# Two transformer layers on one core: waits between PSUM banks of one tile dropped in the first and last stages, and MLP weight blocks loaded through GpSimd's queue

## The chip, the core and the metric

The kernel runs on one core of a Trainium2 chip. In this kernel TensorE (PE in the profile, PEld for its weight loads; 1688.4 us busy in the profile before) multiplies and writes to PSUM. ScalarE (ACT, 1751.8 us) and VectorE (DVE, 1172.0 us) read PSUM and work on SBUF. GpSimd (POOL) is busy for 2.4 us before the change. SyncE (SP) only issues transfers. The metric is the device time of one execution in microseconds, as a median of several executions; lower is better.

## The reference, cut to what matters

```python
x = A_x                                            # 1 x 2048 x 512, bf16
for _ in range(2):                                 # the same weights in both layers
    x = x + attention(layernorm(x), wqkv, wo)      # 32 heads of 16, softmax(q k^T / 4) v
    x = x + relu(layernorm(x) @ w1) @ w2           # 512 -> 1792 -> 512
```

Two layers of attention over 2048 tokens need 2 x 32 x 2048 x 2048 exponentials. They are what most of the time goes to: 1738.8 us of ScalarE in a span of 1836.0 us.

## The kernel before

The kernel plans its own order of instructions while it is being built: `work`, `urgent` and `evac` are lists of pending groups, each with an assumed cost, and the exponentials set the pace. The framework then adds the waits. It knows tiles, not banks: if one engine writes bank 1 of a tile while another still reads bank 0 of it, a wait is put between them (0.67 us of it at 1801.26 us in the profile before).

The kernel has eight banks of PSUM in use, in four tiles. Two tiles `ps_s` of three banks each hold attention scores; `ps_f` and `ps_o` have one bank each. In the first and last stages there are no scores yet, or none left, and those banks serve for everything else:

```python
    wide = [True]
    bank_no = [0]

    def bank():
        if not wide[0]:
            return ps_f[:]
        n = bank_no[0] % 7
        bank_no[0] += 1
        if n == 6:
            return ps_f[:]
        return ps_s[n // W][:, n % W, :]          # W = 3 banks of one tile
```

The first stage (head), after the first layernorm:

```python
    for i in range(TPC):                           # 4 rows of 128 tokens
        pt = ln_transpose(tag, i)                  # 4 TensorE transposes into bank()
        if i % 2:
            nc.scalar.copy(out=xnT[0][:, :, i * P : (i + 1) * P], in_=pt)
        else:
            nc.vector.tensor_copy(out=xnT[0][:, :, i * P : (i + 1) * P], in_=pt)
        mark(("xnT", tag, i))
        idle_matmuls(1)                            # a matmul whose result nobody reads
    ...
    b = plain(k_mms(0, 0))                         # K projection
    nc.scalar.copy(out=ktp[0][0][0][:], in_=b)
    ...
    urgent.append(q_group(None, 0, 0, 0, 0))       # Q projection, two masks on VectorE
    run_all()
    for kb in range(2):                            # V projections
        nc.scalar.copy(out=v_out(0, kb), in_=v_in(plain(v_mms(kb))))
```

In the middle each pair of heads is normalized by this chain. `u` holds 128 x 512 sums; four of its rows are the softmax denominators. They go to a compact tile `c` (8 KB), are inverted, go back into `u`, and are spread to all partitions as `r` (256 KB):

```python
        def copy():                                # u <- ps_o, then
                nc.sync.dma_start(out=c[:], in_=sums)
        def recip():
            nc.vector.reciprocal(out=c[:], in_=c[:])
            nc.sync.dma_start(out=sums, in_=c[:])
            nc.sync.dma_start(out=r[:], in_=bass.AP(tensor=sums.tensor, ...))   # each row 32 times
        def mul(a, w):                             # ot <- u * mask * r
```

The W1 blocks come through SyncE's queue, four buffers deep:

```python
            nc.sync.dma_start(
                out=w1buf[n % NW1][:],
                in_=B_w1[:, ft * P : (ft + 1) * P].rearrange("(c p) f -> p c f", p=P),
            )
```

The last stage (tail), after the last exponential: out-projection of the last 512 tokens, layernorm, transposes, the MLP with 14 W1 groups, store.

```python
    for i in rows:
        last_steps[0](i)
        add(banks[i], ot[NT - 1][:, i * P : (i + 1) * P], wo[:, (NT - 1) // 2, :], False, True)
        nc.scalar.copy(out=x[:], in_=banks[i])
    ...                                            # layernorm
    for i in rows:
        pt = ln_transpose(tag, i, more[i])
        ...                                        # copies to xn2T by both engines
    for ft in range(NF + 1):
        ...                                        # W1 group ft, ReLU, W2 group ft - 1
    for i in rows:
        ...                                        # last copies, stores
```

The softmax here doesn't subtract the row's maximum and nothing guards it: scores larger than these inputs give would overflow.

## Time and profile before

Median 1838.3 us of four runs (1836.8 to 1839.36); the profiled execution has a span of 1836.0 us.

| stretch | from | to | length |
|---|---|---|---|
| head, until the first exponential | 0 | 18.48 | 18.5 us |
| middle, ScalarE full of exponentials | 18.48 | 1781.13 | 1762.7 us |
| tail | 1781.13 | 1836.0 | 54.9 us |

Only time taken out of the head, out of ScalarE's gaps in the middle, or out of the tail counts. The prediction below shows the lines for that. One more view matters for the tail: stretches of the trace cut at the edges where the granted TensorE clock changes. The columns are the stretch and its length, then busy time and instructions of PE, PEld, DVE, ACT and POOL, then the granted clock (1.00 is full), the DMA share and GB/s.

```profile
1795.65:1799.06 3.41, 0.00 (x0) 0.00 (x0) 3.00 (x14) 0.19 (x1) 0.00 (x0) 0.50 0.00 0
1799.06:1802.47 3.41, 1.24 (x9) 0.91 (x10) 2.15 (x8) 0.58 (x1) 0.00 (x0) 0.50 0.00 0
1802.47:1805.89 3.42, 3.20 (x14) 1.74 (x15) 0.42 (x1) 0.58 (x1) 0.00 (x0) 0.50 0.00 0
```

In the traces of the two kernels the clock changes only at edges that lie a whole number of 3.41 us apart (nine changes in each). TensorE stands during the layernorm, in the first stretch. In the second it is busy for just 1.24 us: the transposes are waiting for copies out of neighbouring banks. The third, with 3.20 us of work, is still at half clock; only after it does the clock return (1.00 in the stretch 1805.9 to 1810 us).

### The profile page before, as it was taken

What the parts mean: (1) busy time and instruction counts of PE and PEld (TensorE: products, weight loads), DVE (VectorE), ACT (ScalarE), POOL (GpSimd) and SP (SyncE); (2) the same over time, 40 slices, a digit from 0 to 9 for tenths busy, and PEclk for the clock granted to TensorE, in tenths of its full rate; (3) what the DMA queues carried; (4) which work ended last, traced back from release to release, by engine and by line L of the source; (5) the groups of instructions that cost most, each with busy time, mean ns of one, the idle gap of its engine ahead of it and who ended that gap; (6) DMA issues with size and microseconds to landing.
All of it is one profiled execution on the core that took longest, in us unless ns stands there. A gap on an engine that the chain in (4) does not pass through costs nothing.

```text
span 1836.0 us, 31204 instructions
## 1 busy us (share of the span) xinstructions
PE 1688.4 (92%) x13535; PEld 533.9 (29%) x13709; DVE 1172.0 (64%) x1795; ACT 1751.8 (95%) x1388; POOL 2.4 (0%) x35
## 2 busy tenths in 40 slices
PE   8899999999999999999999888999999999999996
PEld 2223332222232222322222321232222222232223
DVE  7437668677676876778432323586678668666673
ACT  6989999999999999999999997999999999999981
POOL 0000000000000000000000000000000000000000
PEclk9999999999999999999999996999999999999998
DMA  4000000110002000110010001001000110001101
GB/s 144 1 10 11 18 15 8 39 26 11 10 19 46 9 13 11 25 38 13 13 27 15 1 18 27 13 19 42 16 21 8 33 36 16 13 13 41 25 19 40
DMA packets 92749, 42.37 MB, mean 23 GB/s; under 512 B 76612, under 2 KB 84548, under 8 KB 92612
## 3 DMA queue, kind: packets, MB, share of 16 engines
q1 hardware_dynamic: 91268, 39.06, 9.4%
q8 instruction: 107, 1.75, 0.4%
q10 hardware_dynamic: 1344, 1.31, 0.2%
q14 instruction: 30, 0.25, 0.0%
HBM read 20.71 MB, written 2.10 MB: 12 GB/s over the span
## 4 chain that ended last, share of the span: by engine, by line
ACT 82%; PE 11%; DVE 4%; DMA 2%; issue 1%; SPq 0%; DVEq 0%; ACTq 0%
ACT e L934 82%; PE ps_s L911 4%; PE ps_o L701 3%; PE ps_f L360 2%; PE ps_s L984 1%; DMA c<-u 1%; DVE dy L772 1%; DVE di L742 1%; DVE de L772 0%; DMA r<-u 0%; DVE dm L766 0%; DVE q L503 0%; PE ps_f L984 0%; DVE vaug L496 0%; DVE stats L379 0%
## 5 line engine op out<-in xcount | busy, mean ns | idle before, releaser
L934 ACT ACTIVATE e<-ps_s 128x1536 bf16<-128x1536 f32 (+1 forms) x1366 | 1738.8, 1520 | 23.9 <-PE ps_s L911 23.0
L911 PE MATMUL ps_s<-q,ktp 32*128 32x512 bf16 x7287 | 778.2, 384 | 99.2 <-ACT e L934 77.2
L701 PE MATMUL ps_o<-e,vaug 128*32 128x512 bf16 x3860 | 547.0, 393 | 5.6 <-DVE u L647 4.5
L911 PEld LDWEIGHTS <-ktp 32*128 32x128 bf16 x7287 | 232.7, 92 | 530.9 <-issue 460.8
L701 PEld LDWEIGHTS <-vaug 128*32 128x32 bf16 x4568 | 162.8, 93 | 493.5 <-issue 467.1
L742 DVE TENSOR_SCALAR di<-ps_s 128x512 int32<-128x512 f32 x236 | 162.1, 688 | 93.1 <-PE ps_s L911 90.5
L772 DVE SCALAR_TENSOR_TENSOR de<-dy,di 128x1024 bf16<-128x1024 f32 x118 | 144.3, 1223 | 9.1 <-PE ps_o L701 2.4
L772 DVE SCALAR_TENSOR_TENSOR dy<-dm 128x1024 f32<-128x1024 f32 x118 | 144.1, 1221 | 2.5
L772 DVE SCALAR_TENSOR_TENSOR dy<-dy,dm 128x1024 f32<-128x1024 f32 x118 | 144.1, 1221 | 2.1
L545 DVE TENSOR_SCALAR ht<-ps_f 128x512 bf16<-128x512 f32 x98 | 67.5, 689 | 107.8 <-PE ps_f L360 102.0
L360 PE MATMUL ps_f<-xn2T,w 128*128 128x512 bf16 x346 | 114.3, 384 | 5.8 <-issue 1.9
L360 PE MATMUL ps_f<-w,ht 128*128 128x512 bf16 x349 | 110.6, 384 | 4.1 <-issue 3.0
L660 DVE SCALAR_TENSOR_TENSOR ot<-u,mask,r 128x512 bf16<-128x512 f32 (+1 forms) x67 | 46.5, 694 | 69.4 <-DMA r<-u 69.3
L766 DVE TENSOR_SCALAR di<-di 128x1024 int32<-128x1024 int32 x118 | 81.6, 692 | 3.1
L503 DVE TENSOR_SCALAR q<-ps_f,qmask 128x512 bf16<-128x512 f32 x78 | 55.7, 745 | 42.8 <-PE ps_f L360 40.9
L701 PE MATMUL ps_o<-de,vaug 128*32 128x512 bf16 x472 | 82.9, 383 | 0.0
L766 DVE TENSOR_SCALAR dm<-di 128x1024 int32<-128x1024 int32 x118 | 81.3, 689 | 1.5
L360 PE MATMUL ps_f<-xnT,wqkv 128*128 128x512 bf16 x235 | 78.0, 389 | 4.4 <-issue 2.3
L360 PE MATMUL ps_f<-wo,ot 128*128 128x512 bf16 x195 | 63.9, 385 | 2.9 <-issue 2.2
L701 PE MATMUL ps_o<-di,vaug 128*32 128x512 bf16 x236 | 57.7, 391 | 0.0
L649 DVE COPY u<-ps_o 128x512 f32<-128x512 f32 x48 | 33.1, 690 | 30.2 <-PE ps_o L701 30.1
L468 DVE CAST ktp<-ps_f 128x512 bf16<-128x512 f32 x31 | 21.4, 690 | 44.4 <-PE ps_f L360 38.2
(89 smaller groups left out, 517.4 us busy)
## 6 DMA issues: line engine op xcount, KB each, us to landing
r<-u SPq DMA_DIRECT2D x63, 256.0 KB
w<-in_B_w_dram SPq DMA_DIRECT2D x112, 128.0 KB
out_dram<-x SPq DMA_DIRECT2D x16, 128.0 KB
x<-in_A_x_dram SPq DMA_DIRECT2D x14, 128.0 KB
w<-in_B_w_dram SPq DMA_DIRECT2D x1, 1792.0 KB
wqkv<-in_A_wqkv_dram ACTq DMA_DIRECT2D x2, 512.0 KB
c<-u SPq DMA_DIRECT2D x63, 8.0 KB
u<-c SPq DMA_DIRECT2D x63, 8.0 KB
```

The costliest lines, as they stand in the source:

```text
L360: nc.tensor.matmul(b, lhsT, rhs, start=(i == 0), stop=(i == n - 1))
L468: nc.vector.tensor_copy(out=ktp[l][T][j][:], in_=b)
L503: nc.vector.tensor_scalar(out=qbuf[n % 2][e][:], in0=b, scalar1=qmask[e][:, 0:1], scalar2=None, op0=ALU.mult,)
L545: nc.vector.tensor_scalar(out=ht[ft], in0=b, scalar1=0.0, scalar2=None, op0=ALU.max)
L649: nc.vector.tensor_copy(out=u[:], in_=ps_o[:])
L660: nc.vector.scalar_tensor_tensor(out=ot[t][:, a : a + w], in0=u[:, a : a + w], scalar=mask[e][:, 0:1], in1=r[:, a : a + w], op0=ALU.mult, ...
L701: nc.tensor.matmul(ps_o[32 * g : 32 * g + 32, :], vaug[sg["l"]][kb][:, 4 * sg["T"] + g, 2 * e : 2 * e + 32], rhs, start=g not in sg["begun ...
L742: first = nc.vector.tensor_scalar(out=di[:, half, :].bitcast(I32), in0=src, scalar1=EXP_BIAS, scalar2=0.0, op0=ALU.add, op1=ALU.max,)
L766: nc.vector.tensor_scalar(out=out[:].bitcast(I32), in0=di[:].bitcast(I32), scalar1=keep, scalar2=put, op0=ALU.bitwise_and, op1=ALU.bitwise_or,
L772: nc.vector.scalar_tensor_tensor(out=out[:], in0=x[:], scalar=c, in1=y[:], op0=ALU.add, op1=ALU.mult)
L911: nc.tensor.matmul(b[:, w, :], kt[32 * g : 32 * g + 32, kc : kc + P], qbuf[sg["n"] % 2][sg["e"]][32 * g : 32 * g + 32, :], start=True, sto ...
L934: ex = nc.scalar.activation(out=eb[:, :m, :], in_=b[:, :m, :], func=ACTF.Exp, scale=1.0 / (LOG2E * UNIT),)
```

## The change

The intent: drop, in head and tail, the waits between different banks of one tile, and take the 112 W1 loads off SyncE's queue. A helper logs which bank each instruction touches, and tells the framework that an earlier user of another bank of that tile is no dependency. An exception is made where the order comes from data (`needs`). The head's Q projection is written out with the same helper, so the plan of the first 32 us changes a little.

```diff
+    def uses(ins, bank, makes=None, needs=None):
+        tile, w = bank
+        log = users.setdefault(tile, deque(maxlen=40))
+        for other, ow, made_there in log:
+            if (
+                ow != w and other.engine != ins.ins.engine
+                and (needs is None or made_there != needs)
+            ):
+                tc.declare_no_dep(ins.ins, other, reason="different PSUM banks")
+        log.append((ins.ins, w, makes))
...
-            nc.sync.dma_start(
+            nc.gpsimd.dma_start(
                 out=w1buf[n % NW1][:],
...
-        if i % 2:
-            nc.scalar.copy(out=xnT[0][:, :, i * P : (i + 1) * P], in_=pt)
-        else:
-            nc.vector.tensor_copy(out=xnT[0][:, :, i * P : (i + 1) * P], in_=pt)
+        copy = nc.scalar.copy if i % 2 else nc.vector.tensor_copy
+        uses(copy(out=xnT[0][:, :, i * P : (i + 1) * P], in_=pt), in_bank[0], "xnT")
...
-    urgent.append(q_group(None, 0, 0, 0, 0))
-    run_all()
+    b = plain(q_mms(0, 0, 0))
+    for e in range(2):
+        uses(q_masked(0, b, e), in_bank[0])
+    mark(("q", 0))
...
+    wide[0] = True
+    users.clear()
...
-        nc.tensor.matmul(b, lhsT, rhs, start=first, stop=last)
+        uses(nc.tensor.matmul(at_bank(b), lhsT, rhs, start=first, stop=last), b, needs=needs)
...
-        nc.scalar.copy(out=x[:], in_=banks[i])
+        uses(nc.scalar.copy(out=x_t[j * TPC + i][:], in_=at_bank(banks[i])), banks[i], "x")
... (the tail's transposes, ReLUs and last copies in the same way)
```

More of the change, by code (lines that the diff above doesn't have):

```diff
@@ L164 @@
     bank_no = [0]
+    in_bank = [None]
     def bank():
@@ L170, in bank @@
         bank_no[0] += 1
+        in_bank[0] = (2, 0) if n == 6 else (n // W, n % W)
         if n == 6:
@@ L173, in bank @@
         return ps_s[n // W][:, n % W, :]
+    users = {}
+    def uses(ins, bank, makes=None, needs=None):
[8 more added lines that the diff above has]
+        log.append((ins.ins, w, makes))
     now_pe = [0.0]
@@ L413, in ln_apply, with ln_transpose @@
         )
-    def ln_transpose(tag, i, b=None):
+    def ln_transpose(tag, i, b=None, at_bank=None):
         pt = (bank() if b is None else b).bitcast(BF16)
         for c in range(NDC):
-            nc.tensor.transpose(
+            ins = nc.tensor.transpose(
                 pt[:, c * P : (c + 1) * P], xnbuf[i][:, c * P : (c + 1) * P], ident[:]
             )
+            if wide[0]:
+                uses(ins, in_bank[0] if b is None else at_bank)
         mark(("xT", tag, i), "pe")
@@ L499, in v_group, with q_mms, q_masked, q_group @@
         return mm_group(v_mms(kb), fin, [("v", l, kb)], all4("xnT", ("ln1", l, kb // TPC)))
-    def q_group(run, n, l, j, T):
-        def masked(b, e):
-            nc.vector.tensor_scalar(
-                out=qbuf[n % 2][e][:], in0=b, scalar1=qmask[e][:, 0:1], scalar2=None,
-                op0=ALU.mult,
-            )
+    def q_mms(l, j, T):
+        return [(wqkv[:, c, T * P : (T + 1) * P], xnT[j][:, c, :]) for c in range(NDC)]
+    def q_masked(n, b, e):
+        return nc.vector.tensor_scalar(
+            out=qbuf[n % 2][e][:], in0=b, scalar1=qmask[e][:, 0:1], scalar2=None, op0=ALU.mult
+        )
+    def q_group(n, l, j, T):
         def fin(b):
-            masked(b, 0)
-            evac.appendleft((745, 0.0, lambda: (masked(b, 1), mark(("q", n)))))
+            q_masked(n, b, 0)
+            evac.appendleft((745, 0.0, lambda: (q_masked(n, b, 1), mark(("q", n)))))
         return mm_group(
-            [(wqkv[:, c, T * P : (T + 1) * P], xnT[j][:, c, :]) for c in range(NDC)],
-            fin, [("q", n)], all4("xnT", ("ln1", l, j)), cost=745,
+            q_mms(l, j, T), fin, [("q", n)], all4("xnT", ("ln1", l, j)), cost=745
         )
@@ L838, in plain @@
         for i, (lhsT, rhs) in enumerate(mms):
-            nc.tensor.matmul(b, lhsT, rhs, start=(i == 0), stop=(i == len(mms) - 1))
+            ins = nc.tensor.matmul(b, lhsT, rhs, start=(i == 0), stop=(i == len(mms) - 1))
+            uses(ins, in_bank[0], needs="xnT")
         return b
     b = plain(k_mms(0, 0))
-    nc.scalar.copy(out=ktp[0][0][0][:], in_=b)
+    uses(nc.scalar.copy(out=ktp[0][0][0][:], in_=b), in_bank[0])
     mark(("k", 0, 0, 0))
-    urgent.append(q_group(None, 0, 0, 0, 0))
-    run_all()
+    b = plain(q_mms(0, 0, 0))
+    for e in range(2):
+        uses(q_masked(0, b, e), in_bank[0])
+    mark(("q", 0))
     for kb in range(2):
-        nc.scalar.copy(out=v_out(0, kb), in_=v_in(plain(v_mms(kb))))
+        b = plain(v_mms(kb))
+        uses(nc.scalar.copy(out=v_out(0, kb), in_=v_in(b)), in_bank[0])
         mark(("v", 0, kb))
@@ L884 @@
                 if n < len(runs):
-                    urgent.append(q_group(None, n, *runs[n]))
+                    urgent.append(q_group(n, *runs[n]))
             run_until(("q", sg["n"]))
@@ L977, with at_bank, add @@
     rows = range(TPC)
-    free = ps_s[1 - slot[0] % 2]
-    lasts = ps_s[slot[0] % 2]
-    banks = [free[:, w, :] for w in range(W)] + [ps_f[:]]
-    more = [lasts[:, w, :] for w in range(W)] + [ps_o[:]]
-    def add(b, lhsT, rhs, first, last):
-        nc.tensor.matmul(b, lhsT, rhs, start=first, stop=last)
+    last = slot[0] % 2
+    banks = [(1 - last, w) for w in range(W)] + [(2, 0)]
+    more = [(last, w) for w in range(W)] + [(3, 0)]
+    def at_bank(b):
+        n, w = b
+        return ps_s[n][:, w, :] if n < 2 else (ps_f, ps_o)[n - 2][:]
+    def add(b, lhsT, rhs, first, last, needs=None):
+        uses(nc.tensor.matmul(at_bank(b), lhsT, rhs, start=first, stop=last), b, needs=needs)
     for i in rows:
@@ L991 @@
     for i in rows:
-        x = x_t[j * TPC + i]
         last_steps[0](i)
         add(banks[i], ot[NT - 1][:, i * P : (i + 1) * P], wo[:, (NT - 1) // 2, :], False, True)
-        nc.scalar.copy(out=x[:], in_=banks[i])
+        uses(nc.scalar.copy(out=x_t[j * TPC + i][:], in_=at_bank(banks[i])), banks[i], "x")
     for i in rows:
@@ L1002 @@
     for i in rows:
-        pt = ln_transpose(tag, i, more[i])
-        if i % 2:
-            nc.vector.tensor_copy(out=xn2T[:, :, i * P : (i + 1) * P], in_=pt)
-        else:
-            nc.scalar.copy(out=xn2T[:, :, i * P : (i + 1) * P], in_=pt)
+        pt = ln_transpose(tag, i, at_bank(more[i]), more[i])
+        copy = nc.vector.tensor_copy if i % 2 else nc.scalar.copy
+        uses(copy(out=xn2T[:, :, i * P : (i + 1) * P], in_=pt), more[i], "xnT")
     for i in rows:
-        add(banks[i], ident[:], x_t[j * TPC + i][:], True, False)
+        add(banks[i], ident[:], x_t[j * TPC + i][:], True, False, "x")
     for ft in range(NF + 1):
@@ L1014 @@
             for c in range(NDC):
-                add(b, w1buf[n % NW1][:, c, :], xn2T[:, c, :], c == 0, c == NDC - 1)
+                add(b, w1buf[n % NW1][:, c, :], xn2T[:, c, :], c == 0, c == NDC - 1, "xnT")
             if ft % 2:
-                nc.scalar.activation(out=ht[ft], in_=b, func=ACTF.Relu)
+                out = nc.scalar.activation(out=ht[ft], in_=at_bank(b), func=ACTF.Relu)
             else:
-                nc.vector.tensor_scalar(
-                    out=ht[ft], in0=b, scalar1=0.0, scalar2=None, op0=ALU.max
+                out = nc.vector.tensor_scalar(
+                    out=ht[ft], in0=at_bank(b), scalar1=0.0, scalar2=None, op0=ALU.max
                 )
+            uses(out, b, "h")
             load_w1(n + NW1)
@@ L1026 @@
                     banks[i], ht[ft - 1][:, i * P : (i + 1) * P], w2[:, ft - 1, :],
-                    False, ft == NF,
+                    False, ft == NF, "h",
                 )
@@ L1030 @@
         tt = j * TPC + i
-        if i % 2:
-            nc.vector.tensor_copy(out=x_t[tt][:], in_=banks[i])
-        else:
-            nc.scalar.copy(out=x_t[tt][:], in_=banks[i])
+        copy = nc.vector.tensor_copy if i % 2 else nc.scalar.copy
+        uses(copy(out=x_t[tt][:], in_=at_bank(banks[i])), banks[i])
         nc.sync.dma_start(out=out_flat[tt * P : (tt + 1) * P, :], in_=x_t[tt][:])
```

## The prediction

The forecast's sum came to 5.0 us: 2.5 for the head, 0 for the middle, 3.0 for the tail and -0.5 for the loads. The size behind the -0.5 rested on an assumed pace of GpSimd, which no trace before the change shows, and the one chance in six and the 0.5 us were the author's estimate.

> **What bounds the kernel now.** I read the page first (part 1, then part 5), then the list of waits of ScalarE, then the timeline of the first 25 us and of the last 55 us.
>
> ```profile
> PE 1688.4 (92%) x13535; PEld 533.9 (29%) x13709; DVE 1172.0 (64%) x1795; ACT 1751.8 (95%) x1388; POOL 2.4 (0%) x35
> ...
> L934 ACT ACTIVATE e<-ps_s 128x1536 bf16<-128x1536 f32 (+1 forms) x1366 | 1738.8, 1520 | 23.9 <-PE ps_s L911 23.0
> ```
>
> The second line is the exponential of the softmax: 1,366 instructions on ScalarE, busy 1738.8 us, with only 23.9 us of idle time before them. The first one starts at 18.48 us and the last ends at about 1781 us. So the span is a head of 18.5 us, a middle of 1738.8 + 23.9 us that ScalarE fills, and a tail of some 55 us in which no exponential is left. Any gain has to come out of the head, the 23.9 us, or the tail; 2% would be 37 us, more than half of head and tail together.
>
> The head, from the timeline (start, length, engine; in brackets the idle time and what ended it):
>
> ```profile
> 10.96 0.38 PE L418 MATMUL ps_s<-ident,xn 128*128 128x128 bf16 x4 [0.69 <-DVE xnT L829]
> ...
> 12.02 0.38 PE L418 MATMUL ps_s<-ident,xn 128*128 128x128 bf16 x4 [0.46 <-ACT xnT L827]
> ...
> 13.51 1.02 PE L839 MATMUL ps_s<-xnT,wqkv 128*128 128x512 bf16 x4 [0.46 <-ACT xnT L827]
> ...
> 15.21 1.02 PE L360 MATMUL ps_s<-xnT,wqkv 128*128 128x512 bf16 x4 [0.67 <-ACT ktp L843]
> 16.34 1.41 DVE q L503 x2
> ...
> 23.47 24.29 ACT L934 ACTIVATE e<-ps_s 128x1536 bf16<-128x1536 f32 x18 [0.85 <-PE ps_s L911]
> ```
>
> (The fifth line is from the chain that ended last.) Transposes 1 and 2 of the first chunk wait until the copy before them has left another bank of the same three-bank tile ps_s; the Q projection waits for the copy of K out of a neighbouring bank. Only the wait at 13.51, on data, is needed.
>
> The tail:
>
> ```profile
> 1793.31 0.38 PE L984 MATMUL ps_s<-wo,ot 128*128 128x512 bf16 x1 [0.67 <-ACT x L995]
> ...
> 1794.36 0.38 PE L984 MATMUL ps_s<-wo,ot 128*128 128x512 bf16 x1 [0.67 <-ACT x L995]
> ...
> 1801.26 0.59 PE L418 MATMUL ps_s<-ident,xn 128*128 128x128 bf16 x4 [0.67 <-ACT xn2T L1007]
> ...
> 1802.43 0.58 PE L418 MATMUL ps_s<-ident,xn 128*128 128x128 bf16 x4 [0.58 <-DVE xn2T L1005]
> ...
> 1807.30 1.02 PE L984 MATMUL ps_s<-xn2T,w 128*128 128x512 bf16 x4 [0.85 <-DVE ht L1019]
> ...
> 1831.49 0.69 DVE L1032 CAST x<-ps_s 128x512 bf16<-128x512 f32 x1 [3.30 <-ACT x L1034]
> ```
>
> All six are of the same false kind: matmuls held up by a reader of another bank, and in the last line a VectorE copy that waits for a ScalarE copy.
>
> [...] granted clock 0.76 in the stretch 1804 to 1808 us, 1.00 after it, and matmul steps of about 0.43 us against 0.216 us. [...] No transfer of the kernel before goes through GpSimd (its busy time ends at 3 us)[...].
>
> **The change part by part.** First the order of instructions: ScalarE's is identical. TensorE's and VectorE's differ only in the first 147 matmuls and 69 VectorE instructions (up to about 32 us; three redundant score matmuls fewer, the second Q projection earlier), then they are the same to the end. So the middle cannot change by scheduling.
>
> *Head.* After normalisation (10.58 us) the four transposes are then held only by their inputs, which come every 0.35 us from about 9.6: last one done near 11.05, its ScalarE copy (0.58) near 11.7. K starts at 11.7 instead of 13.51: 1.8 us won. Q follows without its 0.67 us wait, after 4 x 0.216 = 0.86 us, and is done near 13.6 instead of 16.25. VectorE has three statistics in front of the Q masks (about 0.8 each from 11.4), so they start near 13.9 instead of 16.34. The exponentials then hang on V: two V groups end near 15.2, three matmuls of the next Q come ahead of the first scores, and scores are ready near 16.3 instead of 18.3. That is 2.0 to 2.2 us. The second Q's masks also come earlier against the exponentials, so the stall of 0.85 us at 23.47 should go: 3.0 us at best. Against it: the four first W1 blocks (512 KB) are now issued at about 3 us instead of 14.6 and share the DMA engines with wqkv. The stretches of the first 20 us show the DMA share at 0.75 to 1.06, 235 to 370 GB/s; 512 KB at 300 GB/s is 1.7 us (my estimate). If all of it fell ahead of V and the x tiles, it would cost about 1 us. I take **2.5 us**.
>
> *Middle.* 0. TensorE never waits for a W1 block: no such line is among the waits. Taking its 112 loads off SyncE's queue (SyncE waits 152.3 and 149.3 us there for TensorE to release the buffers, with the normalising transfers queued behind) can shorten VectorE's 69.3 us of waits for r, but not ScalarE's idle time: nearly all of that lies in 92 to 105 us and 1113 to 1154 us. The second stall starts so:
>
> ```profile
> 1112.54 0.25 DVE L668 RECIPROCAL c<-c 128x16 f32<-128x16 f32 x1 [7.36 <-DMA c<-u]
> ...
> 1117.39 1.45 ACT L934 ACTIVATE e<-ps_s 128x1536 bf16<-128x1536 f32 x1 [3.89 <-PE ps_s L911]
> ```
>
> The transfer c was issued at 1106.21, right behind r; no W1 load is near. TensorE then stands for 3.64 us, the clock halves and some 20 exponentials wait 0.49 us each. I expect all of this again.
>
> *Tail.* (a) Until the second-last row of attention output nothing changes: VectorE waits until 1784.36 for r, issued at 1777.60. (b) The four last out-projection matmuls run back to back; four copies of 0.58 and four statistics of 0.8 follow: the last statistic starts near 1795.7 instead of 1796.21: 0.5. (c) Transposes follow the inputs (0.35 apart) instead of the copies: TensorE is through with them near 1801.2 instead of 1803.44, 2.2 in all. (d) W1 group 1 follows group 0 at once (0.85 saved), and the 0.09 us before groups 5, 9 and 13 goes: 0.3. (e) But TensorE still idles some 5 us in the layernorm, so the clock is still halved, and what is pulled forward runs at 0.43 us a step. If it comes back at 1805.9 as before, about 11 matmuls are done by then and 105 remain: 1805.9 + 105 x 0.216 = 1828.6, against 1830.6: **2.0 us** won. One window earlier it would be 3.7. (f) The last copies start after their own bank's matmul, 0.5 us earlier; the four stores are bound by issue (2.15 us for four), so the rest of what the copies gain is lost: **0.5**. Tail: 2.5 to 4.2, I take **3.0 us**.
>
> *W1 loads in the tail.* On SyncE: issued 1806.47, landed by about 1808.7. On GpSimd a block is asked for at the end of group n and wanted by group n + 4, 4 x 1.725 - 0.86 = 6.0 us later, and one is wanted every 1.725 us. With a latency under 6 us and a pace under 1.7 us it is hidden. Each block is 512 pieces of 256 bytes[...]. I give this one chance in six, 0.5 us on average.
>
> Sum: 2.5 + 3.0 - 0.5 = 5.0 us; 1838.0 - 5.0 = **1833.0 us**.
>
> **Rivals.** (1) *W1 becomes the tail's bound*, as above[...]: for it, 512 pieces a block[...]; against it, four buffers deep[...]. Result 1836 to 1840. (2) *The head is DMA-bound*: W1 delays wqkv so that K or V waits for data; for it, the DMA share near 1 from 6 to 10 us; against it, the 0.75 in 10 to 14 us. Result 1834 to 1836. (3) *The early gain is given back*: up to 105 us TensorE and VectorE have first-layer projections to fit in, and the stalls at 48, 64 and 96 us could grow by what ScalarE gained. Against it, those engines start earlier too. Result about 1835. (4) *The clock changes in the middle*: if the half clock at 1113 us were skipped, 11 us would go: 1822. The stall that sets it off stays, so I give it little.
>
> **Range and chances.** Best cases together give 3.0 + 4.2 = 7.2 us, with a window of clock more about 10; the bad ones about 0 to -1. So 1827 to 1839 should hold it 8 times in 10. Even best it is 0.6%, so "within 2%" is nearly sure.
>
> **What would show it.** K at about 11.7 us and the first exponential between 16.2 and 17.2; no 0.85 us stall near 21; ScalarE's busy time again about 1739 and stalls again near 95 and 1115; in the tail the 0.58 to 0.85 us waits gone, the last matmul some 4.5 us earlier in absolute time, and no wait for W1. Wrong it would be if TensorE waits for w in the tail or the head, if the half clock lasts longer or is missing in the middle[...].

## The result, and the profile after

The changed kernel took 1830.18 us (median of four runs, 1829.28 to 1832.56) against 1838.3 us. The ratio is 0.9958, with a 95% interval of 0.9941 to 0.9976. Here and below a ratio is the mean time of one kernel's fast runs over that of the other's of the same rounds, so it is not quite the ratio of the medians. Predicted were 1833.0 us and a range of 1827 to 1839: the time lies inside it, 2.8 us below the middle. The results of all runs were correct.

The span of the profiled execution fell from 1836.0 to 1828.2 us, 7.8 us. The page of the changed kernel, part 1 and two rows of part 5:

```profile
PE 1684.4 (92%) x13531; PEld 533.0 (29%) x13706; DVE 1172.0 (64%) x1795; ACT 1751.7 (96%) x1388; POOL 86.4 (5%) x147
...
L957 ACT ACTIVATE e<-ps_s 128x1536 bf16<-128x1536 f32 (+1 forms) x1366 | 1738.8, 1517 | 22.1 <-PE ps_s L934 21.3
...
L556 POOL DMA_DIRECT2D w<-in_B_w_dram x112 | 84.0, 750 | 1729.1 <-PE ps_f L378 1594.1
```

ScalarE does the same 1738.8 us of exponentials. GpSimd now spends 0.75 us on each of 112 blocks; the experiments will show no cost of that in the run times. The head of the changed kernel, from its timeline:

```profile
10.42 0.39 PE L436 MATMUL ps_s<-ident,xn 128*128 128x128 bf16 x4
...
10.86 0.39 PE L436 MATMUL ps_s<-ident,xn 128*128 128x128 bf16 x4
...
11.30 0.39 PE L436 MATMUL ps_s<-ident,xn 128*128 128x128 bf16 x4
...
12.36 1.89 PE L858 MATMUL ps_s<-xnT,wqkv 128*128 128x512 bf16 x8 [0.46 <-DVE stats L397]
...
14.28 1.41 DVE L525 TENSOR_SCALAR q<-ps_s,qmask 128x512 bf16<-128x512 f32 x2 [0.17 <-PE ps_s L858]
...
16.99 6.82 ACT L957 ACTIVATE e<-ps_s 128x1536 bf16<-128x1536 f32 x5 [0.40 <-PE ps_s L934]
```

The transposes have no bracket any more, K and Q are one group of eight matmuls, and the first exponential comes at 16.99 instead of 18.48 us. The tail of the changed kernel, from its timeline:

```profile
1788.64 0.81 PE L1012 MATMUL ps_s<-wo,ot 128*128 128x512 bf16 x3
...
1795.85 1.46 PE L436 MATMUL ps_s<-ident,xn 128*128 128x128 bf16 x12 [6.19 <-DVE xn L427]
...
1799.17 1.89 PE L1012 MATMUL ps_s<-xn2T,w 128*128 128x512 bf16 x8
...
1823.28 0.69 DVE L1058 CAST x<-ps_s 128x512 bf16<-128x512 f32 x1 [2.33 <-PE ps_s L1012]
```

Twelve transposes run in one go, two W1 groups too (x8), and the last copy on VectorE waits for a matmul instead of a ScalarE copy. The stretches cut at the clock's edges, for the changed kernel:

```profile
1792.26:1795.67 3.41, 0.00 (x0) 0.00 (x0) 2.92 (x15) 0.00 (x0) 0.00 (x0) 0.50 0.00 0
1795.67:1799.09 3.42, 3.02 (x19) 2.29 (x21) 1.94 (x6) 1.17 (x2) 0.00 (x0) 0.50 0.00 0
```

The stretch right behind the idle one now holds 3.02 us of TensorE work instead of 1.24, and the clock returns after it: two stretches at half clock instead of three.

Where the 7.8 us of this pair of traces came from:

| stretch | before | after | won |
|---|---|---|---|
| head: start of the sixth exponential | 26.15 | 24.19 | 1.96 us |
| middle: from there to the end of the last exponential | 1754.98 | 1753.32 | 1.66 us |
| tail: from there to the end | 54.87 | 50.69 | 4.18 us |

### The profile page after: what moved, and what is told of

Same layout as the page of the kernel before. It is cut to its first block, busy times and chain, and to the rows that moved or that the text cites. A ratio compares the mean times of both kernels' runs of the same rounds, so it can differ in the third digit from the quotient of the medians.

```text
span 1828.2 us, 31187 instructions
## 1 busy us (share of the span) xinstructions
PE 1684.4 (92%) x13531; PEld 533.0 (29%) x13706; DVE 1172.0 (64%) x1795; ACT 1751.7 (96%) x1388; POOL 86.4 (5%) x147
## 4 chain that ended last, share of the span: by engine, by line
ACT 82%; PE 11%; DVE 4%; DMA 2%; issue 1%; DVEq 0%; SPq 0%
ACT e L957 82%; PE ps_s L934 4%; PE ps_o L722 3%; PE ps_f L378 3%; PE ps_s L1012 1%; DMA c<-u 1%; DVE dy L793 1%; DVE di L763 1%; DVE de L793 0%; DMA r<-u 0%; DVE dm L787 0%; DVE vaug L516 0%; DVE stats L397 0%; PE ps_f L1012 0%; DVE ktp L488 0%
## 5 line engine op out<-in xcount | busy, mean ns | idle before, releaser
L957 ACT ACTIVATE e<-ps_s 128x1536 bf16<-128x1536 f32 (+1 forms) x1366 | 1738.8, 1517 | 22.1 <-PE ps_s L934 21.3
L556 POOL DMA_DIRECT2D w<-in_B_w_dram x112 | 84.0, 750 | 1729.1 <-PE ps_f L378 1594.1
L681 DVE SCALAR_TENSOR_TENSOR ot<-u,mask,r 128x512 bf16<-128x512 f32 (+1 forms) x67 | 46.5, 694 | 71.1 <-DMA r<-u 70.9
```

The source lines that it names most:

```text
L556: nc.gpsimd.dma_start(out=w1buf[n % NW1][:], in_=B_w1[:, ft * P : (ft + 1) * P].rearrange("(c p) f -> p c f", p=P),)
L681: nc.vector.scalar_tensor_tensor(out=ot[t][:, a : a + w], in0=u[:, a : a + w], scalar=mask[e][:, 0:1], in1=r[:, a : a + w], op0=ALU.mult, ...
L957: ex = nc.scalar.activation(out=eb[:, :m, :], in_=b[:, :m, :], func=ACTF.Exp, scale=1.0 / (LOG2E * UNIT),)
```

## The experiments

The questions: which part of the change brings the gain, why the tail gave more than predicted, whether the middle's 1.66 us is real, and what the loads do. The last runs turn to the stall that both kernels keep.

### The loads alone, and the waits alone

```diff
# e1: the kernel before, load_w1          # e2: the changed kernel, load_w1
-            nc.sync.dma_start(           -            nc.gpsimd.dma_start(
+            nc.gpsimd.dma_start(         +            nc.sync.dma_start(
```

> The kernel before with only the W1 loads moved to GpSimd's queue. Theory (the dropped waits carry the gain, the loads nothing): 1838 us, within 1.5 us of the kernel before, first exponential at 18.5 to 18.8 us, ScalarE's idle time before the exponentials 24 us. Rival (taking the loads off SyncE's queue shortens the normalising transfers): 1836 us or less, and VectorE's waits for r well under 69 us.

> The changed kernel with the W1 loads back on SyncE's queue. Theory: 1830 us, within 1.5 us of the changed kernel; first exponential near 17.0 us, last one ending near 1777.5 us, end of the tail some 50.7 us after that. Rival (loads carry a part): 1833 us or more.

e1 took 1838.89 us, ratio 1.0003 (0.9988 to 1.0018). e2 took 1830.17 us, ratio 0.9958 (0.9943 to 0.9972), the same as the whole change. So the dropped waits bring the gain, and the loads neither give nor cost anything that these times show. In the changed kernel a block lands a median of 2.6 us after its issue, and the list of TensorE's waits has none for `w`. VectorE's waits did not shrink in it either: 70.9 us for `r` against 69.3 in the kernel before, 37.6 us for `c` against 37.2.

### The head alone, the tail alone

```diff
+    drop = [True]                        # e3, the head alone; [False] for e4, the tail alone
     def uses(ins, bank, makes=None, needs=None):
+        if not drop[0]:
+            return
...
     wide[0] = True                       # the tail begins
     users.clear()
+    drop[0] = False                      # e3; True for e4
```

> The changed kernel with the waits between banks kept in the tail. Theory (head and tail are separate terms): last exponential ends near 1777.5 us as in the changed kernel, then a tail of about 54.9 us as before: 1834.4 us. If the gain of the middle (1.65 us) hangs on the head's shift, it is here too. Rival (the tail's gain needs nothing of the head's, and the head's is lost on the way): last exponential at 1780 us or later, 1836 us.

> The changed kernel with the waits between banks kept in the head (its order of instructions kept). Theory: first exponential near 18.5 us, the last one ends at 1780 to 1781.5 us, the tail is 50.7 to 52 us: 1832.5 to 1834.5 us. If the new order of the head alone were the cause of the head's gain, the first exponential would come near 17 us and the time would be 1830 us.

e3 took 1835.6 us, ratio 0.9987 (0.997 to 1.0004); e4 took 1833.39 us, ratio 0.9975 (0.9961 to 0.999). Against 1837.69 us for the kernel before on that chip these are 2.1 and 4.3 us, 6.4 in sum, where both together give 7.5 (e2, on the same chip). The intervals are about 3 us wide on each side, so the two parts add up as far as this can be seen; that of e3 reaches just past 1, so by time alone the head's part is not clear of noise. The tail is the larger part. The tails in the traces are 55.17 us in e3 and 50.40 us in e4: as before, and as after.

Two expectations fell. In e3 the last exponential ended at 1779.22 us, not near 1777.5. In e4 the first exponential came at 21.10 us, not near 18.5:

```profile
14.00 1.87 PE L861 MATMUL ps_s<-xnT,wqkv 128*128 128x512 bf16 x4 [0.25 <-ACT xnT L851]
...
21.10 1.45 ACT L960 ACTIVATE e<-ps_s 128x1536 bf16<-128x1536 f32 x1 [0.40 <-PE ps_s L937]
```

The waits between banks are back in it (0.68, 0.46 and 0.67 us), but that is not all. The K projection takes 1.87 us here instead of 1.02: in this execution the clock was halved in the head too, for two steps, from 11.34 to 18.17 us. So this trace does not show what the new order of the head costs by itself. The profiled executions of e5 and e6 below had one such step (from 10.78 and from 11.10 us), with the first exponential at 17.76 and 18.03 us.

### The tail's transposes, and the rest of the tail

Both keep the head of the changed kernel. In e5 only the waits around the tail's transposes are dropped; in e6 all but those. The edit is the same flag, switched around the loop of `ln_transpose`.

> The changed kernel, in whose tail only the waits around the four transposes are dropped (the head is as changed). Theory (the tail won 4.2 us instead of 3.0 because the transposes and identity matmuls now follow each other closely enough for the clock to come back one window earlier): two half-clock windows in the layernorm stretch instead of three, tail 51 to 52.5 us. Rival (the window depends on the back-to-back first MLP groups, or on where the grid of windows falls): three windows, tail 53 to 54.5 us.

> The changed kernel, in whose tail the waits around the four transposes are kept and all others dropped. Theory: three half-clock windows, tail 53 to 54 us (0.5 of the statistics, 0.5 of the last copies, 0.3 to 1 of the MLP groups won). Rival: two windows, tail 51 to 52 us.

e5 took 1833.87 us (0.9977, 0.9963 to 0.9992), e6 1833.15 us (0.9974, 0.9957 to 0.999): by time they can't be told apart. The traces can (a half-clock window is one 3.41 us step at half clock):

| kernel | tail | half-clock windows in the layernorm |
|---|---|---|
| before | 54.87 us | 3 |
| e1, loads only | 55.31 | 3 |
| e3, head only | 55.17 | 3 |
| e6, all but the transposes | 53.26 | 3 |
| e5, only the transposes | 52.91 | 2 |
| after | 50.69 | 2 |
| e2, waits only | 50.58 | 2 |
| e4, tail only | 50.40 | 2 |

In these eight traces the third half-clock window is there exactly where the transposes keep their waits. The rival of e5, that it hangs on where the grid of windows falls, is out: the first of these windows begins 14.3 to 15.0 us after the last exponential in all eight (why so evenly is told below, under the middle). The window that fills up in the trace after holds the 16 transposes and three matmuls with the identity; which of these the clock answers to was not separated. e5 won 2.0 us of tail and e6 1.6 us, against 4.2 us for both; e5's 52.91 us is just above its expected 51 to 52.5.

### Keeping TensorE busy in the tail

```diff
# e8: the changed kernel; idle_matmuls(n) are n matmuls whose result nobody reads
+            if (i, t) == (0, NT - 2):     # while the second-last attention rows are awaited
+                idle_matmuls(8)
...
+    idle_matmuls(24)                      # ahead of the tail's transposes
```

> The changed kernel with 8 idle matmuls in the tail's wait for r and 24 in its layernorm, so that TensorE's clock is not halved there. Theory (the half clock costs the tail some 2 us: steps of 0.43 instead of 0.216 us in the out-projection and at the identity matmuls): no half clock in the tail before its end, tail 48 to 49 us, 1828 us. Rival (VectorE and the copies set the pace there, not TensorE): tail 50 us or more, 1830 us.

e8 took 1828.67 us, ratio 0.9949 (0.9934 to 0.9964), 1.5 us below the changed kernel by medians of two jobs; the intervals of the two ratios overlap, so the evidence is the trace. It has no half clock in the tail until 1827.9 us, when the work is done; the tail is 47.69 us, 3.0 less than after. So half clock still costs the tail of the changed kernel some 3 us; its three half-clock windows of 3.41 us would cost 5.1 us (an estimate, half of 3 x 3.41 us) if TensorE's work filled them all, which it doesn't (0.00 us in the second).

### A transfer on another queue: a miss

Both kernels stall at about 1113 us, where VectorE waits over 7 us (7.36 before, 7.35 after) for the 8 KB of `c`, queued on SyncE behind the 256 KB of `r`. e7 moves the small one:

```diff
-                nc.sync.dma_start(out=c[:], in_=sums)
+                nc.gpsimd.dma_start(out=c[:], in_=sums)
```

> The changed kernel with the transfer of the row sums (c from u, 63 of them) on GpSimd's queue instead of SyncE's. Theory (that transfer is slow, 6.3 us for 8 KB, because it stands behind the 256 KB of r in SyncE's rings, and this wait stops TensorE for 3.6 us and halves the clock for 11 or 12 windows): c lands in under 3 us, no stall and no half clock from 1110 to 1154 us, ScalarE's idle time before the exponentials 8 us instead of 22, 1816 us. Rival (the transfer is slow by itself, four short reads into 128 partitions, or W1 loads now stand before it): the stall stays, 1830 us.

e7 took 1829.5 us, ratio 0.9948 (0.9926 to 0.9969): as the changed kernel. One of its four executions took only 1822.76 us, at a mean clock of 0.991 against 0.986 to 0.987 in the others. It was not the profiled one, so which half-clock time it was spared is not known. The transfer itself did what was hoped at this place: VectorE's wait for `c` fell from 7.35 to 2.59 us. `c` lands in a median of 2.1 us, but in 6.9 at worst, and all of VectorE's waits for `c` together fell only from 37.6 to 33.5 us. The timeline of e7 shows what came in its place:

```profile
1112.31 0.75 DVE L681 SCALAR_TENSOR_TENSOR ot<-u,mask,r 128x512 bf16<-128x512 f32 x1 [4.60 <-DMA r<-u]
...
1115.02 0.62 PE L722 MATMUL ps_o<-e,vaug 128*32 128x512 bf16 x4 [3.64 <-DVE u L668]
...
1117.08 1.45 ACT L957 ACTIVATE e<-ps_s 128x1536 bf16<-128x1536 f32 x1 [3.89 <-PE ps_s L934]
```

VectorE now waits 4.60 us for `r`, the next transfer in the chain, and TensorE and ScalarE stand exactly as long as in the kernel before (3.64 and 3.89 us). The bound was the chain of transfers, not the one of them named by the wait.

### The spreading transfer replaced: first a miss, then the best kernel

VectorE can spread a row to the partitions of a group (STREAM_SHUFFLE, 723 ns for 128x512 in e11), and is idle 36% of the time (1172.0 us busy of 1828.2). e9 uses it instead of the 256 KB transfer:

```diff
             nc.vector.reciprocal(out=c[:], in_=c[:])
             nc.sync.dma_start(out=sums, in_=c[:])
-            nc.sync.dma_start(out=r[:], in_=bass.AP(tensor=sums.tensor, ...))
-            mark(("r", n), lag=8500.0)                  # what the plan assumes, in ns
+            mark(("r", n), lag=2600.0)
...
-            task(700, lambda: mul(0, QS), ots + [("m", n)], [("r", n)] + war)
+            def spread_mul():
+                nc.vector.stream_shuffle(out=r[:], in_=u[:], mask=[lane] * 32)
+                mul(0, QS)
+            task(1400, spread_mul, ots + [("m", n)], [("r", n)] + war)
```

> The changed kernel with the transfer that spreads the row sums to all partitions (6.6 us for 256 KB in the trace after) replaced by a VectorE stream_shuffle, so that nothing of the normalization waits for a transfer but the 8 KB of c. Theory (the stall and the half clock around 1110 to 1154 us come from VectorE waiting for c behind r on one queue, and the half clock costs some 20 exponentials 0.49 us each): c lands in about 2 us, no half clock there, the last exponential 10 to 13 us earlier, time about 1816 to 1820. Rival (the shuffles, some 63 of about 0.7 us, put VectorE behind on eviction and a new wait takes their place): a stall of 2 us or more at the same place, a half clock again, time 1828 to 1840.

> The same with the idle matmuls of the run e8 in the tail. Theory: the two are independent, so 1.5 us below the run e9_shuffle. Rival: the tail is already without half clock or bound by VectorE, and the time is that of e9_shuffle within 0.5 us.

e9 took 1841.17 us, ratio 1.0015 (0.9999 to 1.0032), and e10 1840.62 us (1.0011, 0.9996 to 1.0026). The idle matmuls added nothing that the intervals show (0.5 us by the medians). The stall at 1113 us was gone, as the theory had it, but others had come at 545, 769 and 931 us. The worst of them in the timeline of e9:

```profile
922.24 0.45 PE L436 MATMUL ps_f<-ident,xn 128*128 128x128 bf16 x4 [2.87 <-DVE xn L427]
...
927.54 1.87 PE L378 MATMUL ps_f<-xnT,wqkv 128*128 128x512 bf16 x4 [0.51 <-DVE xnT L471]
...
929.34 0.60 PE L931 MATMUL ps_s<-q,ktp 32*128 32x512 bf16 x1
...
930.90 1.45 ACT L954 ACTIVATE e<-ps_s 128x1536 bf16<-128x1536 f32 x1 [11.56 <-PE ps_s L931]
```

Here the layernorm, transposes and K projection of the next layer stand bare on the path, one after the other, while no scores are left to exponentiate: ScalarE waits 11.56 us. I had told the kernel's planner the true, shorter lag of `r`. It packed the instructions anew, and the new order was worse. The edit had two parts, and the second hid the first.

e11 and e12 therefore keep the planner's old figures (`lag=8500.0`, `task(700, ...)`), though they no longer describe the transfer. By the listing of instructions, TensorE, ScalarE and GpSimd then have exactly the order of the changed kernel, and VectorE 63 shuffles more.

> The run e9_shuffle removed the stall at 1110 to 1154 us, but its scheduler, told of other costs, packed the instructions anew, and new stalls of up to 11.56 us came at 543, 769 and 931 us. Here the 63 shuffles take the place of the transfers with the scheduler's figures left as they were, so that TensorE, ScalarE and GpSimd have exactly the order of the changed kernel and VectorE only 63 instructions more (by the listing of instructions). Theory: the stall at about 1113 us goes, with its 11 or 12 windows of half clock, and no other comes, since VectorE is busy 64% of the time and gets 46 us more; the last exponential about 10 to 13 us earlier, time 1815 to 1820. Rival (VectorE needs the time that the transfers gave it, each shuffle delays what TensorE waits for): new stalls, ScalarE's idle time before the exponentials 20 us or more, time 1828 or above.

> The same with the idle matmuls of the run e8 in the tail. Theory: the two are independent and both stand, so 1.5 to 3 us below e11_shuffle_order. Rival: within 0.5 us of it.

e11 took 1814.63 us (1813.54 to 1815.5), ratio 0.9874 (0.9857 to 0.989); e12 took 1813.94 us, ratio 0.987 (0.9855 to 0.9885). The page of e11, two rows, and stretches of its trace around the old stall:

```profile
L957 ACT ACTIVATE e<-ps_s 128x1536 bf16<-128x1536 f32 (+1 forms) x1366 | 1737.8, 1518 | 10.9 <-PE ps_s L934 9.9
...
L709 DVE STREAM_SHUFFLE r<-u 128x512 f32<-128x512 f32 x63 | 45.6, 723 | 0.0
```

```profile
1100.00:1110.00 10.00, 8.97 (x87) 2.97 (x87) 3.75 (x7) 10.00 (x8) 0.00 (x0) 1.00 0.02 2
1110.00:1120.00 10.00, 8.60 (x90) 3.11 (x88) 3.18 (x7) 10.00 (x9) 0.00 (x0) 1.00 0.03 4
```

ScalarE is busy for all of both stretches, the clock is full, and its idle time in front of the exponentials is 10.9 us instead of 22.1. From the first exponential to the end of the last, e11 takes 1748.3 us against 1760.5 after: 12.2 us. The tail gives 2.7 us more (48.04 us against 50.69), and its half-clock window at 1782 us, in which `r` was awaited, is gone. The idle matmuls of e12 bring 0.7 us by the medians, which the intervals can't tell from nothing: the theory of 1.5 us or more fell. e11's tail is already within 0.5 us of the tails with the idle matmuls (48.04 us; 47.60 in e12 and 47.69 in e8).

## Why the prediction was right or wrong

**Total.** The terms were 2.5 for the head, 0 for the middle, 3.0 for the tail and -0.5 for the loads. The profiled pair shows 2.0, 1.7, 4.2 and (e1, e2) nothing for the loads. The mechanism was right, and three sizes were off. That the time lies in the stated range says little by itself, for 1827 to 1839 us holds the kernel before (1838.3 us) too; what speaks for the prediction is that the waits it named are gone, one by one, in the trace after.

**Head, 2.5 predicted, 2.0 measured.** The step that failed is "K starts at 11.7". It started at 12.36. Of the 0.66 us between, 0.30 is the later arrival of x (first statistics at 3.78 instead of 3.48 us). Counted from there, 10.03 us became 8.58: 1.45 us won instead of 1.8. The transposes follow each other at 0.44 us (10.42, 10.86, 11.30), not at the inputs' 0.35. Between them stands the idle matmul, at 0.216 us: four transposes and one idle matmul take 0.44 us. I had left it out of the sum because it does no work. The first exponential came 1.49 us earlier, where 2.0 to 2.2 were forecast. The stall of 0.85 us did not quite go either: brackets of 0.40 and 0.38 us stand in its place. The fear that the earlier W1 loads would delay the head came true in part: in six traces (e3, e7 to e10 and e12) the V projection waits 0.23 to 0.86 us for wqkv. From e8:

```profile
14.34 1.02 PE L858 MATMUL ps_f<-wqkv,xnT 128*128 128x512 bf16 x4 [0.73 <-DMA wqkv<-in_A_wqkv_dram]
```

The trace after and that of e11 have no such wait, nor has e2, which has the early head and the loads on SyncE. Whether the loads or the earlier V projection bring it, one trace of e2 can't decide.

**Middle, 0 predicted, 1.7 in this pair.** The order of instructions is the same on ScalarE, and both stalls came again, as predicted:

```profile
1109.48 0.25 DVE L689 RECIPROCAL c<-c 128x16 f32<-128x16 f32 x1 [7.35 <-DMA c<-u]
...
1113.76 1.45 ACT L957 ACTIVATE e<-ps_s 128x1536 bf16<-128x1536 f32 x1 [3.30 <-PE ps_s L934]
```

What the step overlooked is that the half clock behind the stall ends on an edge of a 3.41 us grid. It ended at 1153.95 us before and at 1150.56 us after, one window apart, and the last exponential ended 627.2 and 626.9 us behind that edge. In nine of ten traces (of the two kernels and e1 to e8) this distance is 626.7 to 627.4 us. So in these traces what the head wins is rounded to whole windows in one execution, and where the grid lies differs from execution to execution: e2 and the changed kernel start their exponentials at 16.83 and 16.99 us, and end them at 1779.22 and 1777.51. The 1.7 us are luck of this pair, not a gain of the change: the same stretch took 1754.89 us in e3, with the changed head, and 1753.36 us in e1, with the old one. e7 is the trace that falls out of the nine, at 628.1. In medians the head alone is worth 2.1 us (e3), which is the head's own size, though its interval does not exclude a gain of zero. The scatter of 2 to 3 us between executions goes with the clock too: of the 28 executions of the kernel before in these jobs, those with a mean clock of 0.982 took 1837.6 to 1839.7 us, those with 0.983 1836.5 to 1838.4, the two with 0.985 1835.2 and 1835.4.

**Tail, 3.0 predicted, 4.2 measured.** Counted from the end of the exponentials (3.62 us earlier in this trace), the steps are:

- (b) statistics 0.5 predicted; the last one starts at 1792.09 instead of 1796.21, 4.12 - 3.62 = 0.5. Right.
- (c) transposes 2.2 in all; the first W1 group starts at 1799.17 instead of 1804.95, 5.78 - 3.62 = 2.2. Right.
- (e) "If it comes back at 1805.9 as before" failed. The clock returned at 1799.09, which is 6.8 us earlier by the trace's own time, or one window earlier once the window by which the middle had moved is taken off. In absolute time the last matmul came 7.3 us earlier where the prediction expected 4.5. It starts at 1823.30 instead of 1830.62: 7.32 - 3.62 = 3.7 us won, the very number that the prediction gave for one window earlier, and not 2.0. This is the mis-sized term, and the table of eight traces shows its cause: with the transposes' waits gone, TensorE fills the first window after the layernorm (3.02 us of 3.42) where it had filled 1.24 of 3.41. The prediction had moved work forward, and held the clock fixed. In this tail the clock follows the work; in the middle full windows did not bring it back. In the changed kernel TensorE, with matmuls mostly of 32\*128 and 128\*32 there, was busy 13.23 us of the 13.70 from 1119.80 us on, and the half clock went on until 1150.56 us, 11 windows in all (12 in the kernel before). What decides that stays open.
- (f) last copies 0.5; 4.18 - 3.70 = 0.5. Right.

**Loads, -0.5 predicted, 0 measured.** The chance of one in six that GpSimd would be too slow did not come: 0.75 us of issue for a block that is wanted every 1.725 us. Nor did VectorE's instructions become longer: its busy time is 1172.0 us in both traces.

**The rivals.** W1 as the tail's bound is excluded by e1 and e2. A head bound by transfers showed as a wait of under 1 us in six traces (above). The early gain was not given back. A changed clock in the middle was right in kind (its windows decide the middle), but the large gain it named, 11 us, was not to be had from this change; e11, which took the stall away at its root, got 12.2 us there.

## What to carry to other kernels

Where one tile spans several PSUM banks, look for matmuls that wait for a copy out of a neighbouring bank: the dropped waits were worth some 8 us here, all of it in the head and tail, where ScalarE does not set the pace. When work is pulled forward next to an idle gap, ask whether it now fills the first clock window behind the gap (in this tail one full window was enough, 3.02 us of 3.42; in the middle 13.23 us of 13.70 were not). Here the clock changed with the schedule (two half-clock windows in the layernorm instead of three, and full clock around 1113 us in e11), so the estimate that held it fixed was off. And when a wait is cured by moving one transfer, look at what is next in its chain (e7), and change the mechanism without the planner's figures first (e9 against e11): the same replacement gave 1841 or 1815 us depending on the order alone.
